# Attention and two gated layers on one core: query tiles through one copied bank, first transfers by a list

## The chip, the core and the metric

The kernel runs on one core of a Trainium2 chip. A core has TensorE (matmuls, which write to PSUM), VectorE, ScalarE and GpSimd (elementwise work; GpSimd works on SBUF), and SyncE, whose queue issues the transfers between HBM and SBUF here. The metric is the device time of one execution in microseconds (us). The profile calls the engines PE (PEld is its weight load), DVE, ACT, POOL and SP.

## What is computed

```
kv  = einsum('bhsd,bhse->bhde', k, v)            # 4 batches, 8 heads, 576 tokens, 64 wide
out = einsum('bhsd,bhde->bhse', q, kv)
x   = out / sqrt(mean(out * out, axis=-1) + 1e-06) * g_norm   # as 2304 tokens x 512
x   = ((x @ w_a) * (x @ w_b)) @ w_out                         # 512 -> 1536 -> 512
y   = (sigmoid(x @ w_gate) * (x @ w_val)) @ w_out2            # the same sizes
```

All data are float32. There is no softmax, so keys and values shrink to a 64 x 64 matrix for each head and batch before a query is needed.

## The kernel before

**Attention.** Keys and values come in 16 transfers of 640 KB, four pieces for each of four batches; a piece (two heads) is five matmuls into a quarter of a PSUM bank (L405). When a batch's four pieces are done, the two diagonal blocks of the bank are copied into `kvbd`, one by ScalarE (L416), one by VectorE (L419). Queries come as 18 tiles of 128 tokens, 256 KB each. A query tile is four or eight matmuls against `kvbd` (L475). ScalarE squares the result (L484), VectorE sums it by heads (L491), and once a *lot* of two or three tiles has its sums, GpSimd, ScalarE and VectorE make the inverse root from them (L436, L440, L443, L449 to L453). VectorE multiplies the tile in PSUM by it (`xn`, L497), TensorE transposes it (L504), and ScalarE copies it into `part` (L510), the SBUF tensor that holds x for the layers that follow.

**The layers.** Tokens go in three groups of 768, weights in quarters of two blocks of 128 columns (12 blocks a layer). For each group and quarter there are seven *kinds* of products (a Strassen form; kinds 1 to 7), each for the two factors u and v, six matmuls of 384 columns (L549); then eight output projections of six matmuls (L641), whose results are added into `part` by VectorE (L649, or by copies L651 and L653 in the first quarter). A product needs x or a sum of parts of x (L324) split in a high and a low part (L343 on ScalarE, L346 on GpSimd or VectorE), and weights that are clamped, rounded and split in the same way (load L225; L234, L238, L242 to L254; L290, L294). Split x is stored to HBM (L350) and reloaded for later quarters (L363).

**PSUM.** Six banks u0 to u5 are for products; o0 and o1 are for everything else. Query tiles 0 to 11 use u0 to u5, tiles 12 to 17 use o0 and o1; keys and values and transposes use o1 (transposes from tile 12 on o0 or o1); output projections use o0 and o1 in turn.

**What sets the order.** Every step is an `op` of a `Plan` with an engine, a planned duration, the steps that it needs (`after`), buffers that it takes (`new`) and uses, and a due time. `order` works due times back from the products, whose due times are a fixed grid 1,044 ns apart, then walks through time and gives each free engine the ready step that is due first. The list that comes out is the program: each engine runs its steps in that order. The transfers of SP run in order as well, and one that waits for its buffer holds those behind it. At most eight transfers are under way, since the ninth waits for the first to land. Three rings of buffers matter: `xr` (five, split x and the keys and values in flight), `q` (three query tiles) and `raw` (two weight blocks as they arrive).

Of the kernel before, what the change touches and what calls it, by code (L numbers as in the profile page):

```python
# [16 lines left out]
ACTF = mybir.ActivationFunctionType  # L17
# [31 lines left out]
         "gf": 2, "q": 3, "xn": 2, "ss": 2, "rr": 2}  # L49
# [4 lines left out]
LOTS = [(0, 1, 2), (3, 4, 5), (6, 7, 8), (9, 10, 11), (12, 13), (14, 15), (16, 17)]  # L54


class Plan:
# [6 lines left out]
    def op(self, name, eng, ns, fn, after=(), new=(), uses=(), due=None, lag=150, port=False):  # L64
        o = dict(name=name, eng=(eng,) if isinstance(eng, str) else eng, ns=ns, fn=fn, new=list(new),
                 uses=list(uses) + [b for _, b in new], due=due, lag=lag, port=port, succ=[], need=0, at=None)
        self.by[name] = o
        o["after"] = list(after)
        self.ops.append(o)

    def order(self):
# [21 lines left out]
        free_at = {e: 0 for e in ("PE", "DVE", "ACT", "POOL", "SP")}  # L93
        ready = {e: [] for e in free_at}
# [3 lines left out]
        events = [(0, i, "ready", o) for i, o in enumerate(ops) if not o["need"]]  # L98
# [69 lines left out]
def attention_then_two_moes(  # L168
# [49 lines left out]
    W_DUE = {(0, "a"): 17e3, (0, "b"): 17e3, (1, "a"): 20e3, (1, "b"): 20e3}  # L218

    def weights(F, which):  # L220
# [38 lines left out]
        op(("load", k), "SP", dma(512), load, new=[("raw", raw)], due=W_DUE.get(k), lag=2000)  # L259
# [122 lines left out]

    def keys_values(b):
        bank = ("K", b)
        for p in range(KC):
            kv = ("kv", b, p)

            ring = b < 2 or p > 1

            def load(p=p, kv=kv, ring=ring):  # L390
                if ring:
                    t = new_tile("xr", [2, 2, N])
                    t = t.rearrange("p a c n -> p (a c n)")
                else:
                    t = part[b - 1][:, p].rearrange("p k n -> p (k n)")
# [12 lines left out]

            op(kv, "SP", dma(640), load, (), [("xr", kv)] if ring else [], lag=2000)
            op(("K", b, p), "PE", 1120, mm, [kv] + ([("K", b, p - 1)] if p else [("O", t) for t in tiles_of.get(b - 2, ())]),  # L410
               [("o1", bank)] if p == 0 else [], ([bank] if p else []) + ([kv] if ring else []))
# [10 lines left out]
        op(("V", b, 0), "ACT", 400, up, before, uses=[bank])  # L422
        op(("V", b, 1), "DVE", 430, dn, before, uses=[bank])

# [36 lines left out]
    def queries(t):  # L461
        q = ("q", t)
        bank, tbank = ("O", t), ("T", t)
        tag, ttag = f"u{t % 6}" if t < 12 else f"o{t % 2}", f"o{t % 2}" if t >= 12 else "o1"

        def load():
            x = new_tile("q", [KC * P])
# [26 lines left out]

        def norm():
            tl["xn", t] = new_tile("xn", [KC, P])
            V.tensor_tensor(  # L497
                out=heads(tl["xn", t]), in0=heads(tl[bank]), in1=tl["rr", lot][:, t - lot[0]].to_broadcast([P, H, D]), op=ALU.mult
            )

        def transpose():
            b = tl[tbank] = bank_of(ttag).rearrange("p (k n) -> p k n", k=KC)
# [6 lines left out]
        def to_x():  # L509
# [3 lines left out]
        op(q, "SP", dma(256), load, (), [("q", q)], due=18e3 if t < 3 else None, lag=2000)  # L513
        op(bank, "PE", 1000, mm, [q] + [("V", i, e) for i, _, _ in batches(t) for e in (0, 1)]
           + ([('T', t - 2)] if t >= 12 else []), [(tag, bank)], [q])
# [6 lines left out]
        op(xn, "DVE", 720, norm, [rr], [("xn", xn)], [bank, rr])  # L522
        op(tbank, "PE", 480, transpose, [xn], [(ttag, tbank)], [xn])
        op(("Y", t), "ACT", 700, to_x, [tbank, "gcol"] + ([("K", in_part[t][0] + 1, in_part[t][1])] if t > 5 else []),
# [143 lines left out]
    op("gcol", "SP", 100, lambda: nc.sync.dma_start(out=gcol, in_=g_col), lag=2000)  # L668
# [89 lines left out]
```

## Time and profile before

| | |
|---|---|
| median of 3 runs | 931.04 us (930.25 to 932.25) |
| profiled execution | 927.02 us, span 925.2 us |
| PE busy | 890.8 us, 96% of the span |
| DVE, ACT, POOL busy | 638.0, 423.4, 334.5 us |
| HBM | 256 MB, 277 GB/s over the span |

The span is the stretch from the first to the last instruction of the program in the trace; the execution's own time is a little longer. Times in the rows count from the span's start. A matmul in float32 appears as two records, so ten records are a piece of keys and values; a few records can be missing. A row of the timeline merges neighbours of one kind: start, length, engine, line, what it writes and reads, how often, and in brackets the idle time ahead of it with what ended that.

### The profile page before, as it was taken

The page shows a single profiled execution, that of the slowest core. Times are in us where ns is not written, and L with a number is a line of the kernel's source. Part 1 is how long each engine was busy: PE and PEld are TensorE (multiplying, and loading weights), DVE is VectorE, ACT ScalarE, POOL GpSimd, SP SyncE. Part 2 cuts the span into 40 slices and gives each one's busy share as a digit, 9 for nine tenths or more (in the row PEclk, how much of TensorE's full clock was granted, in tenths as well). Part 3 has the DMA queues.
Part 4 walks back from the last instruction along what each step waited for, and adds up shares of the span by engine and source line. Part 5 has one row for each costly group of instructions (what it writes and reads, how often), then busy time and mean ns, then how long its engine had stood idle before and what let it go on. Part 6 is the DMA issues. An engine that isn't in the chain of part 4 may idle for free.

```text
span 925.2 us, 14091 instructions
## 1 busy us (share of the span) xinstructions
PE 890.8 (96%) x5144; PEld 882.6 (95%) x5144; DVE 638.0 (69%) x1129; ACT 423.4 (46%) x812; POOL 334.5 (36%) x307
## 2 busy tenths in 40 slices
PE   5889789999999999999999999999999999999998
PEld 5878779999999999999999999999999999999998
DVE  5588878578766766766778798777667667644445
ACT  4476555444443343343346575554444444333321
POOL 3245454234413413323336554332322322311111
PEclk8999989999999999999999999999999999999999
DMA  8795649988887787787785678988787797777783
GB/s 351 265 367 223 211 178 318 372 308 303 306 311 272 258 308 261 267 325 268 262 326 213 244 270 300 337 328 285 264 320 266 263 326 261 242 237 239 243 286 120
DMA packets 55221, 256.78 MB, mean 278 GB/s; under 512 B 6256, under 2 KB 9328, under 8 KB 55152
## 3 DMA queue, kind: packets, MB, share of 16 engines
q1 hardware_dynamic: 55152, 255.88, 77.4%
q8 instruction: 41, 0.67, 0.3%
q14 instruction: 28, 0.23, 0.1%
HBM read 218.10 MB, written 37.75 MB: 277 GB/s over the span
## 4 chain that ended last, share of the span: by engine, by line
PE 87%; DMA 5%; DVE 3%; POOL 1%; issue 1%; ACT 1%; SPq 0%; POOLq 0%; ACTq 0%
PE ps_u L549 54%; PE ps_o L641 32%; DMA raw<-w_all_dram 4%; DMA xr<-kv_in_dram 1%; PE ps_u L475 1%; PE ps_o L405 1%; DVE s L324 1%; DVE xn L497 1%; DMA x<-xr 0%; PE ps_o L504 0%; DVE mag L244 0%; POOL xr L346 0%; ACT xr L343 0%; DVE xr L346 0%; ACT mag L234 0%
## 5 line engine op out<-in xcount | busy, mean ns | idle before, releaser
L549 PE MATMUL ps_u<-xr,wp 128*128 128x384 f32 x3024 | 554.3, 336 | 2.7 <-ACT xr L343 1.1
L549 PEld LDWEIGHTS ps_u<-xr,wp 128*128 128x128 f32 x3024 | 529.3, 188 | 4.1 <-POOL xr L346 1.4
L641 PE MATMUL ps_o<-gu,wo 128*128 128x384 f32 x864 | 199.5, 339 | 11.2 <-DVE xn L497 9.4
L641 PE MATMUL ps_o<-gv,wo 128*128 128x384 f32 x864 | 201.4, 341 | 0.0
L649 DVE TENSOR_TENSOR part<-ps_o,part 128x384 f32<-128x384 f32 x240 | 132.0, 554 | 88.1 <-PE ps_o L641 87.6
L641 PEld LDWEIGHTS ps_o<-gu,wo 128*128 128x128 f32 x864 | 155.8, 190 | 13.6 <-DVE xn L497 6.6
L641 PEld LDWEIGHTS ps_o<-gv,wo 128*128 128x128 f32 x864 | 157.8, 190 | 0.0
L621 POOL TENSOR_TENSOR gu<-gf,gu 128x384 fp32r<-128x384 f32 x53 | 56.3, 1062 | 273.4 <-ACT gu L618 223.3
L254 POOL TENSOR_TENSOR w<-mag,last 128x512 int32<-128x512 int32 x72 | 97.7, 1362 | 109.3 <-DVE mag L248 106.0
L234 ACT ACTIVATE mag<-raw 128x512 f32<-128x512 f32 x72 | 48.2, 669 | 74.2 <-DMA raw<-w_all_dram 60.8
L294 POOL TENSOR_TENSOR wp<-tmp,wp 128x512 fp32r<-128x512 f32 x28 | 37.5, 1344 | 96.5 <-ACT wp L290 96.1
L618 ACT ACTIVATE gu<-gf 128x384 fp32r<-128x384 f32 x72 | 37.6, 522 | 63.6 <-DVE gf L614 63.3
L242 DVE TENSOR_SCALAR mag<-mag 128x512 f32<-128x512 f32 x72 | 35.2, 489 | 36.5 <-ACT mag L234 36.5
L248 DVE SCALAR_TENSOR_TENSOR mag<-raw,mag 128x512 uint32<-128x512 uint32 x72 | 49.9, 695 | 0.8
L290 ACT ACTIVATE wp<-tmp 128x512 fp32r<-128x512 f32 x48 | 30.2, 629 | 44.0 <-PE ps_u L549 26.3
L238 ACT ACTIVATE last<-raw 128x512 int32<-128x512 uint32 x72 | 47.6, 662 | 0.0
L567 ACT ACTIVATE u2u<-ps_u 128x384 f32<-128x384 f32 x36 | 17.6, 488 | 64.9 <-PE ps_u L549 64.9
L290 ACT ACTIVATE wp<-w 128x512 fp32r<-128x512 f32 (+1 forms) x48 | 24.9, 521 | 44.5 <-PE ps_u L549 35.0
L294 POOL TENSOR_TENSOR wp<-w,wp 128x256 fp32r<-128x256 f32 (+1 forms) x30 | 30.0, 1001 | 39.8 <-ACT wp L290 39.7
L618 ACT ACTIVATE gv<-gf 128x384 fp32r<-128x384 f32 x72 | 37.6, 522 | 14.2 <-DVE gf L614 13.9
L346 POOL TENSOR_TENSOR xr<-s,xr 128x768 fp32r<-128x768 f32 x16 | 31.1, 1945 | 33.3 <-ACT xr L343 30.7
L244 DVE TENSOR_SCALAR mag<-mag 128x512 uint32<-128x512 uint32 x72 | 40.7, 566 | 2.5
(78 smaller groups left out, 833.0 us busy)
## 6 DMA issues: line engine op xcount, KB each, us to landing
xr<-x SPq DMA_DIRECT2D x210, 768.0 KB, 5.9
raw<-w_all_dram SPq DMA_DIRECT2D x72, 512.0 KB, 5.7
x<-xr SPq DMA_DIRECT2D x42, 768.0 KB, 4.0
xr<-kv_in_dram SPq DMA_DIRECT2D x12, 640.0 KB, 7.2
q<-q_t_dram SPq DMA_DIRECT2D x18, 256.0 KB, 5.4
out_dram<-part SPq DMA_DIRECT2D x24, 192.0 KB, 2.2
part<-kv_in_dram SPq DMA_DIRECT2D x4, 640.0 KB, 6.3
gcol<-g_col_dram SPq DMA_DIRECT2D x1, 0.5 KB, 4.9
```

The costliest lines, as they stand in the source:

```text
L234: A.activation(out=tl["mag", k], in_=words(1).bitcast(F32), func=ACTF.Abs, scale=65536.0)
L238: A.activation(out=tl["last", k], in_=words(0), func=ACTF.Copy, scale=2.0**-29)
L244: V.tensor_scalar(out=m, in0=m, scalar1=3, scalar2=None, op0=ALU.logical_shift_left)
L248: V.scalar_tensor_tensor(out=m, in0=words(1), scalar=0x80000000, in1=m, op0=ALU.bitwise_and, op1=ALU.bitwise_or)
L254: G.tensor_tensor(out=tl["w32", k].bitcast(I32), in0=tl["mag", k].bitcast(I32), in1=tl["last", k], op=ALU.add)
L290: A.activation(out=tl[name][:, 0, :], in_=tl[src][:, cut], func=ACTF.Copy)
L294: eng.tensor_tensor(out=t[:, 1, :], in0=tl[src][:, cut], in1=t[:, 0, :], op=ALU.subtract)
L549: nc.tensor.matmul(out=o, lhsT=wt[:, a, c], rhs=x[:, b, k, :], start=(i in "152" and k == 0 and (a, b) == (0, 0)), stop=(k == 1 and (a, b) ...
L618: A.activation(out=tl[name][:, 0, :], in_=tl[me, "gf", t], func=ACTF.Copy)
L621: eng.tensor_tensor(out=tl[name][:, 1, :], in0=tl[me, "gf", t], in1=tl[name][:, 0, :], op=ALU.subtract)
L641: nc.tensor.matmul(out=o[:, :N], lhsT=tl["wo", f_of(g, uv)][:, a, c], rhs=tl["g", g, uv, t][:, b, :], start=(uv, a, b) == mms[0], stop=(uv ...
L649: V.tensor_tensor(out=acc, in0=o, in1=acc, op=ALU.add)
```

## The change

Four things are done. **First**, query tiles from the seventh on (t = 6 to 17) go through bank o0 alone; ScalarE copies the result out of PSUM into an `xn` buffer (of which there are four instead of two), and VectorE's multiplication then works in that buffer. Transposes all use o1. Lots are of two from the seventh tile on. **Second**, query tiles 0 to 5 are loaded into `part[0]`, which is not needed until x is written there, and all keys and values of batches 2 and 3 into `part[1]` and `part[2]`. **Third**, a list `FIRST` gives the first transfers their order by a `rank`, which overrides the due time: batch 0 in four pieces, four query tiles, the first two weight blocks, batch 1, two query tiles, two weight blocks, and so on. **Fourth**, both diagonal blocks are copied by ScalarE.

```diff
-LOTS = [(0, 1, 2), (3, 4, 5), (6, 7, 8), (9, 10, 11), (12, 13), (14, 15), (16, 17)]
+LOTS = [(0, 1, 2), (3, 4, 5), (6, 7), (8, 9), (10, 11), (12, 13), (14, 15), (16, 17)]
...
+        for o in ops:
+            if o["rank"] is not None:
+                o["due"] = o["rank"]
...
-    W_DUE = {(0, "a"): 17e3, (0, "b"): 17e3, (1, "a"): 20e3, (1, "b"): 20e3}
+    FIRST = [("kv", 0, p) for p in range(KC)] + [("q", t) for t in range(4)]
+    FIRST += [("load", (0, c)) for c in "ab"] + [("kv", 1, p) for p in range(KC)] + [("q", 4), ("q", 5)]
+    FIRST += [("load", (1, c)) for c in "ab"] + ["gcol"] + [("kv", 2, p) for p in range(KC)]
+    FIRST += [("q", t) for t in range(6, 9)] + [("kv", 3, p) for p in range(KC)]
+    load_due = {name: 100 * i - 1e5 for i, name in enumerate(FIRST)}
...
-            ring = b < 2 or p > 1
+            ring = b < 2
+            place = (1, p) if (b, p) in ((2, 0), (2, 1)) else (2, p % 2)
...
-        def up():
-            A.activation(out=dst[0:64, :, 0:64], in_=tl[bank][0:64, :, 0:64], func=ACTF.Copy)
-        def dn():
-            V.tensor_copy(out=dst[64:128, :, 64:128], in_=tl[bank][64:128, :, 64:128])
+        def diagonal():
+            for h in range(2):
+                r = slice(64 * h, 64 * h + 64)
+                A.activation(out=dst[r, :, r], in_=tl[bank][r, :, r], func=ACTF.Copy)
...
-        tag, ttag = f"u{t % 6}" if t < 12 else f"o{t % 2}", f"o{t % 2}" if t >= 12 else "o1"
+        tag = f"u{t}" if t < 6 else "o0"
...
+            if t < 6:
+                x = part[0][:, t // 3].rearrange("p k n -> p (k n)")[:, t % 3 * KC * P:(t % 3 + 1) * KC * P]
+            else:
+                x = new_tile("q", [KC * P])
...
+        def copy():
+            tl["xn", t] = new_tile("xn", [KC, P])
+            A.activation(out=tl["xn", t], in_=tl[bank], func=ACTF.Copy)
...
-        op(xn, "DVE", 720, norm, [rr], [("xn", xn)], [bank, rr])
+        if t < 6:
+            op(xn, "DVE", 720, norm, [rr], [("xn", xn)], [bank, rr])
+        else:
+            op(("copy", t), "ACT", 610, copy, [bank], [("xn", xn)], [bank])
+            op(xn, "DVE", 720, norm, [rr, ("copy", t)], (), [xn, rr], port=True)
```

Line numbers move: L405 becomes L419, L475 L491, L497 L519, L504 L526, L510 L532, L549 L576, L641 L668, the copy out of PSUM is L514.

The new order moves nearly every instruction; three places follow. On TensorE, where the first group's projections (L641, into the banks `ps_o`) meet the last query tiles (`ps_o<-kvbd,q`), the order before is:

```order
L549 MATMUL ps_u_935<-xr,wp_245 128x384 x6
L641 MATMUL ps_o_1135<-gu_776,wo 128x384 x3
L641 MATMUL ps_o_1135<-gv_808,wo 128x384 x3
L641 MATMUL ps_o_1149<-gu_776,wo 128x384 x3
L641 MATMUL ps_o_1149<-gv_808,wo 128x384 x3
L504 MATMUL ps_o_1162<-ident,xn 128x128 x4
L641 MATMUL ps_o_1170<-gu_776,wo 128x384 x3
L641 MATMUL ps_o_1170<-gv_808,wo 128x384 x3
L475 MATMUL ps_o_1184<-kvbd_66,q 128x128 x4
L504 MATMUL ps_o_1193<-ident,xn 128x128 x4
L475 MATMUL ps_o_1204<-kvbd_66,q 128x128 x4
```

And in the order after, at the same projections:

```order
L668 MATMUL ps_o_912<-gu_743,wo 128x384 x3
L668 MATMUL ps_o_912<-gv_824,wo 128x384 x3
L526 MATMUL ps_o_925<-ident,xn 128x128 x4
L668 MATMUL ps_o_934<-gu_743,wo 128x384 x3
L668 MATMUL ps_o_934<-gv_824,wo 128x384 x3
L526 MATMUL ps_o_949<-ident,xn 128x128 x4
L491 MATMUL ps_o_961<-kvbd_66,q 128x128 x4
L668 MATMUL ps_o_970<-gu_743,wo 128x384 x3
L668 MATMUL ps_o_970<-gv_824,wo 128x384 x3
```

The projections, which stood in blocks, now alternate with single transposes and query tiles. On ScalarE, around the first copies of transposed tiles into `part_67` (that is `part[0]`), the order before alternates squares (`sq`) and copies:

```order
L484 ACTIVATE sq<-ps_u_396 128x512
L510 ACTIVATE part_67<-ps_o_403,gcol 128x4x128
L484 ACTIVATE sq<-ps_u_412 128x512
L510 ACTIVATE part_67<-ps_o_423,gcol 128x4x128
L484 ACTIVATE sq<-ps_u_430 128x512
L510 ACTIVATE part_67<-ps_o_450,gcol 128x4x128
```

After, the first three copies (L532) stand among the steps of the first weights (`mag`, `last`, `wp`):

```order
L298 ACTIVATE wp_267<-w_246 128x256
L242 ACTIVATE mag<-raw 128x512
L500 ACTIVATE sq<-ps_u_271 128x512
L246 ACTIVATE last<-raw 128x512
L242 ACTIVATE mag<-raw 128x512
L532 ACTIVATE part_67<-ps_o_259,gcol 128x4x128
L500 ACTIVATE sq<-ps_u_285 128x512
L246 ACTIVATE last<-raw 128x512
L532 ACTIVATE part_67<-ps_o_309,gcol 128x4x128
L298 ACTIVATE wp_333<-tmp 128x512
L298 ACTIVATE wp_336<-w_320 128x512
L452 ACTIVATE root<-ss 128x24
```

The next entry there is the third copy, so five, two and three entries stand ahead of the three copies. On SP, the transfers around the first reloads of split x (`xr<-x_...`; `x_...<-xr` are the stores, `raw` the weights) stand before as:

```order
L225 DMA raw<-w_all_dram 128x512
L350 DMA x_1213<-xr 128x1536
L225 DMA raw<-w_all_dram 128x512 x4
L350 DMA x_1395<-xr 128x1536
L350 DMA x_1415<-xr 128x1536
L350 DMA x_1442<-xr 128x1536
L350 DMA x_1464<-xr 128x1536
L363 DMA xr<-x_569 128x1536
```

And after:

```order
L358 DMA x_1395<-xr 128x1536
L358 DMA x_1414<-xr 128x1536
L371 DMA xr<-x_432 128x1536
L371 DMA xr<-x_576 128x1536
L371 DMA xr<-x_597 128x1536
L358 DMA x_1514<-xr 128x1536
L233 DMA raw<-w_all_dram 128x512
L371 DMA xr<-x_664 128x1536
L233 DMA raw<-w_all_dram 128x512
```

The two `raw` loads of the lower piece (the last blocks of the second quarter's weights) are the first two of the four that stood ahead of the reloads before.

## Rows read from the trace of the kernel before

**Rows 1.** Windows: stretch in us, busy time and instructions by engine, granted clock, DMA

```profile
5.00:10.00 5.00, 2.23 (x10) 1.93 (x10) 3.23 (x5) 2.69 (x5) 1.30 (x1) 1.00 1.04 414
18.50:25.30 6.80, 6.04 (x28) 6.05 (x29) 3.13 (x6) 1.52 (x3) 2.30 (x2) 0.50 0.62 238
85.00:103.80 18.80, 14.14 (x88) 13.28 (x87) 16.63 (x26) 8.53 (x16) 9.57 (x15) 1.00 0.72 262
103.80:107.20 3.40, 3.40 (x14) 3.30 (x13) 2.55 (x7) 1.77 (x4) 0.85 (x1) 0.51 0.10 39
117.50:124.30 6.80, 5.11 (x16) 5.11 (x17) 3.37 (x7) 2.79 (x5) 3.16 (x5) 0.50 0.10 38
130.00:925.20 795.20, 790.01 (x4510) 788.24 (x4508) 547.79 (x982) 350.85 (x682) 278.30 (x226) 1.00 0.79 280
```

**Rows 2.** Waits of PE, whole span: us in total, times, longest

```profile
PE ps_o L405 <- DMA xr<-kv_in_dram: 10.2, 5, 4.7
PE ps_o L641 <- DVE xn L497: 9.4, 3, 4.7
...
PE ps_o L641 <- DVE part L649: 1.6, 2, 1.1
...
PE ps_o L641 <- ACT part L651: 0.2, 1, 0.2
```

**Rows 3.** Timeline of PE, 99 to 150 us

```profile
103.22 0.78 PE L641 MATMUL ps_o<-gu,wo 128*128 128x384 f32 x3 [3.42 <-DVE xn L497]
...
119.19 1.33 PE L641 MATMUL ps_o<-gu,wo 128*128 128x384 f32 x3 [4.74 <-DVE xn L497]
...
131.90 4.50 PE L549 MATMUL ps_u<-xr,wp 128*128 128x384 f32 x24
...
146.75 8.51 PE L549 MATMUL ps_u<-xr,wp 128*128 128x384 f32 x48
```

**Rows 4.** Timeline of PE, the first 45 us

```profile
4.72 2.50 PE L405 MATMUL ps_o<-xr 128*128 128x128 f32 x10 [4.72 <-DMA xr<-kv_in_dram]
10.89 4.49 PE L405 MATMUL ps_o<-xr 128*128 128x128 f32 x20 [3.66 <-DMA xr<-kv_in_dram]
...
26.26 1.28 PE L405 MATMUL ps_o<-xr 128*128 128x128 f32 x10
27.37 1.06 PE L475 MATMUL ps_u<-kvbd,q 128*128 128x128 f32 x8
28.27 1.28 PE L405 MATMUL ps_o<-xr 128*128 128x128 f32 x10
...
42.91 0.66 PE L504 MATMUL ps_o<-ident,xn 128*128 128x128 f32 x4
43.41 2.16 PE L475 MATMUL ps_u<-kvbd,q 128*128 128x128 f32 x16
```

**Rows 5.** Groups of instructions of the first 128 us: busy us, mean ns | idle

```profile
L254 POOL TENSOR_TENSOR w<-mag,last 128x512 int32<-128x512 int32 x11 | 16.0, 1455 | 29.7 <-DVE mag L248 29.6
L510 ACT ACTIVATE part<-ps_o,gcol 128x512 f32<-128x512 f32 x18 | 12.3, 686 | 8.8 <-PE ps_o L504 8.7
L491 DVE TENSOR_REDUCE ss<-sq 128x8 f32<-128x512 f32 x18 | 12.3, 682 | 8.8 <-ACT sq L484 8.8
...
L416 ACT ACTIVATE kvbd<-ps_o 64x256 f32<-64x256 f32 x4 | 1.5, 372 | 5.3 <-PE ps_o L405 5.3
```

**Rows 6.** Timeline of DVE, 29 to 64 us

```profile
29.10 0.69 DVE L491 TENSOR_REDUCE ss<-sq 128x8 f32<-128x512 f32 x1
...
33.42 0.69 DVE L497 TENSOR_TENSOR xn<-ps_u,rr 128x512 f32<-128x512 f32 x1 [0.21 <-POOL rr L453]
...
54.87 1.97 DVE L346 TENSOR_TENSOR xr<-part,xr 128x768 fp32r<-128x768 f32 x1 [0.57 <-ACT xr L343]
...
62.77 0.95 DVE L346 TENSOR_TENSOR xr<-part,xr 128x768 fp32r<-128x768 f32 x1
```

**Rows 7.** Timeline of POOL, 50 to 58 us

```profile
54.19 1.84 POOL L346 TENSOR_TENSOR xr<-s,xr 128x768 fp32r<-128x768 f32 x1 [1.77 <-ACT xr L343]
```

More of the change, by code (lines that the diff above doesn't have):

```diff
@@ L62, in __init__, with op @@
         self.ops, self.by, self.n = [], {}, 0
-    def op(self, name, eng, ns, fn, after=(), new=(), uses=(), due=None, lag=150, port=False):
+    def op(self, name, eng, ns, fn, after=(), new=(), uses=(), due=None, lag=150, port=False, rank=None):
         o = dict(name=name, eng=(eng,) if isinstance(eng, str) else eng, ns=ns, fn=fn, new=list(new),
-                 uses=list(uses) + [b for _, b in new], due=due, lag=lag, port=port, succ=[], need=0, at=None)
+                 uses=list(uses) + [b for _, b in new], due=due, lag=lag, port=port, rank=rank, succ=[], need=0, at=None)
         self.by[name] = o
@@ L97, in order @@
         tag_of = {b: tag for tag, bs in turn.items() for b in bs}
-        events = [(0, i, "ready", o) for i, o in enumerate(ops) if not o["need"]]
+        events = [(1300, i, "ready", o) for i, o in enumerate(ops) if not o["need"]]
         heapq.heapify(events)
@@ L381, in bank_of @@
         return ps.tile([P, 512], F32, tag=tag, name=f"ps_{tag}")
+    at_part = {}
     def keys_values(b):
@@ L386, in keys_values, with load @@
             kv = ("kv", b, p)
-            ring = b < 2 or p > 1
-            def load(p=p, kv=kv, ring=ring):
+            ring = b < 2
+            place = (1, p) if (b, p) in ((2, 0), (2, 1)) else (2, p % 2)
+            before = [("K", *at_part[place])] if place in at_part else []
+            if not ring:
+                at_part[place] = (b, p)
+            def load(p=p, kv=kv, ring=ring, place=place):
                 if ring:
@@ L394, in load @@
                 else:
-                    t = part[b - 1][:, p].rearrange("p k n -> p (k n)")
+                    t = part[place[0]][:, place[1]].rearrange("p k n -> p (k n)")
                 t = t[:KP, :KJ * 2 * P]
@@ L407, in mm @@
                     )
-            op(kv, "SP", dma(640), load, (), [("xr", kv)] if ring else [], lag=2000)
-            op(("K", b, p), "PE", 1120, mm, [kv] + ([("K", b, p - 1)] if p else [("O", t) for t in tiles_of.get(b - 2, ())]),
+            op(kv, "SP", dma(640), load, () if ring else before, [("xr", kv)] if ring else [], rank=load_due[kv], lag=2000)
+            op(("K", b, p), "PE", 1200, mm, [kv] + ([("K", b, p - 1)] if p else [("O", t) for t in tiles_of.get(b - 2, ())]),
                [("o1", bank)] if p == 0 else [], ([bank] if p else []) + ([kv] if ring else []))
         dst = kvbd[b % 2]
-        def up():
-            A.activation(out=dst[0:64, :, 0:64], in_=tl[bank][0:64, :, 0:64], func=ACTF.Copy)
-        def dn():
-            V.tensor_copy(out=dst[64:128, :, 64:128], in_=tl[bank][64:128, :, 64:128])
+        def diagonal():
+            for h in range(2):
+                r = slice(64 * h, 64 * h + 64)
+                A.activation(out=dst[r, :, r], in_=tl[bank][r, :, r], func=ACTF.Copy)
         before = [("K", b, 3)] + [("O", t) for t in tiles_of.get(b - 2, ())]
-        op(("V", b, 0), "ACT", 400, up, before, uses=[bank])
-        op(("V", b, 1), "DVE", 430, dn, before, uses=[bank])
+        op(("V", b), "ACT", 700, diagonal, before, uses=[bank])
     def powers(lot):
@@ L493, in mean @@
             )
+        def copy():
+            tl["xn", t] = new_tile("xn", [KC, P])
+            A.activation(out=tl["xn", t], in_=tl[bank], func=ACTF.Copy)
         def norm():
-            tl["xn", t] = new_tile("xn", [KC, P])
+            if t < 6:
+                tl["xn", t] = new_tile("xn", [KC, P])
             V.tensor_tensor(
-                out=heads(tl["xn", t]), in0=heads(tl[bank]), in1=tl["rr", lot][:, t - lot[0]].to_broadcast([P, H, D]), op=ALU.mult
+                out=heads(tl["xn", t]), in0=heads(tl[bank] if t < 6 else tl["xn", t]), in1=tl["rr", lot][:, t - lot[0]].to_broadcast([P, H, D]), op=ALU.mult
             )
         def transpose():
-            b = tl[tbank] = bank_of(ttag).rearrange("p (k n) -> p k n", k=KC)
+            b = tl[tbank] = bank_of("o1").rearrange("p (k n) -> p k n", k=KC)
             for p in range(KC):
@@ L512, in queries @@
         sq, xn, ss, rr = (("sq", t), ("xn", t), ("ss", lot), ("rr", lot))
-        op(q, "SP", dma(256), load, (), [("q", q)], due=18e3 if t < 3 else None, lag=2000)
-        op(bank, "PE", 1000, mm, [q] + [("V", i, e) for i, _, _ in batches(t) for e in (0, 1)]
-           + ([('T', t - 2)] if t >= 12 else []), [(tag, bank)], [q])
+        op(q, "SP", dma(256), load, (), [] if t < 6 else [("q", q)], rank=load_due.get(q), lag=2000)
+        op(bank, "PE", 1000, mm, [q] + [("V", i) for i, _, _ in batches(t)]
+           + ([('T', t - 4)] if t >= 10 else []), [(tag, bank)],
+           [] if t < 6 else [q])
         op(sq, "ACT", 610, square, [bank], [("sq", sq)], [bank])
@@ L521, in queries @@
             powers(lot)
[L522 to L524 removed]
+        if t < 6:
+            op(xn, "DVE", 720, norm, [rr], [("xn", xn)], [bank, rr])
+        else:
+            op(("copy", t), "ACT", 610, copy, [bank], [("xn", xn)], [bank])
+            op(xn, "DVE", 720, norm, [rr, ("copy", t)], (), [xn, rr], port=True)
+        op(tbank, "PE", 480, transpose, [xn], [("o1", tbank)], [xn])
+        op(("Y", t), "ACT", 700, to_x, [tbank, "gcol"] + ([("K", *at_part[in_part[t]])] if t > 5 else [("O", i) for i in range(6)]),
            uses=[tbank])
@@ L665, in down @@
                [("sum", g, t, d)], lag=2000)
-    op("gcol", "SP", 100, lambda: nc.sync.dma_start(out=gcol, in_=g_col), lag=2000)
+    op("gcol", "SP", 100, lambda: nc.sync.dma_start(out=gcol, in_=g_col), rank=load_due["gcol"], lag=2000)
     for b in range(B):
```

6 lines of the change are left out of this document (3 added, 3 removed).

## The prediction

> **What bounds the kernel now.** I read the windows first, then TensorE's waits and its timeline, and last the engines that it waits for. From 130 us to the end TensorE is busy 790.01 of 795.20 us at the full clock [rows 1]: those 795 us are a queue of matmuls almost without holes, and only the opening can become shorter. In the list of waits the reader should see two causes behind most of TensorE's idle time: keys and values still in flight (10.2 us) and, three times, an output projection (L641) that waits for the attention's normalised tile xn (9.4 us) [rows 2].
>
> A fixed point makes the opening countable. In both orders the same 94 pieces of TensorE work stand ahead of the first product of kind 5 of the third token group: 16 key-value pieces, 18 query tiles, 18 tiles of transposes, 30 products and 12 output projections. Since what follows has hardly a hole, the time at which that product starts moves the end by as much. Before, it starts at 131.90 us [rows 3]. Unit times without a wait: 48 matmuls, which are 8 products, take 8.51 us, 1.06 each [rows 3] (a projection has as many); a key-value piece takes 27.37 - 26.26 = 1.11, a query tile 28.27 - 27.37 = 0.90, a tile of transposes 43.41 - 42.91 = 0.50 [rows 4]. The work is 16 x 1.11 + 18 x 0.90 + 18 x 0.50 + 42 x 1.06 = 87.5 us, so 131.9 - 87.5 = 44.4 us are lost.
>
> Where they go. Idle: the 13 rows of the list add up to 31.0, of which the 1.6 behind L649 come later, so 29.4 us [rows 2]. Clock: three stretches at 1.2 GHz hold 6.04, 3.40 and 5.11 us of busy TensorE, half of it lost, 7.3 us [rows 1]; the second and the third follow waits of 3.42 and 4.74 us [rows 3]. Besides, the first three key-value pieces took 2.50 + 4.49 us where three take 3.33 later, 3.7 us lost [rows 4]. That is 40.4; the other 4.0 are gaps too short for the list.
>
> **The change part by part.**
>
> *First transfers in order.* Before, the later pieces of batch 0 stand behind weights and queries, and TensorE waits 3.66 us for the second [rows 4]. Now the four pieces go first. The queue moves 414 GB/s [rows 1], so 640 KB land every 1.58 us after the first at 4.7 us. At 6.99 / 3 = 2.33 us a piece TensorE no longer waits between them, but still loses half of three: 4.7 us idle and 3.7 of clock (2.4 to 4.9 for two to four pieces). Batch 0 is done at 4.7 + 6.99 + 1.11 = 12.8.
>
> *Both diagonal blocks on ScalarE.* Two copies of 0.37 in a row [rows 5] instead of one there and one on VectorE beside it: 0.75 us until the first query tile at 13.55; the fourth ends at 17.2. Batch 1's last piece comes after 6,528 KB more, at 4.7 + 16.1 = 20.8, and is done at 21.9; 0.3 us are lost to data.
>
> *First norms.* VectorE now has steps of the weights between the sums of squares. Three sums are 2.0 us [rows 5], and two clamp pairs with a sign step 3.23, as the five VectorE entries of 5 to 10 us show [rows 1]. The first square ends at 13.55 + 0.90 + 0.7 = 15.1, so the third sum at 20.4. From such a sum's end to its xn the trace has 33.42 - 29.79 = 3.6 us, and xn takes 0.69 [rows 6]: transposes from 24.6, 2.7 us lost.
>
> *Three transposes through one bank.* Each needs ScalarE's copy of the one before, 0.69 us [rows 5], and now ScalarE has weights and squares ahead of it: five entries before the first copy, two before the second, three before the third, as the order shows, and one of the last waits for a GpSimd add of 1.46 [rows 5]. Ten entries of 0.22 to 0.67, 5.7 us in all, with three copies and the add make 9.2: the third copy ends at 33.8. TensorE has three transposes and two query tiles in that time, 3.3 us; 5.9 are lost, 2.1 if every copy were prompt. With so little work the clock should fall there. The three stretches of before cost 1.7 to 3.0 each; I take 2.5.
>
> *From there to the first long wait.* TensorE waits 0.7 for the diagonal copies, twice 0.6 for copies out of PSUM, 1.0 for a copy into part: each is one or two ScalarE entries. Then products need part of x: behind the sixth transposes come copy, norm, sum, high part and GpSimd's low part, 1.84 [rows 7], the other four under 1 us each, some 5.6 together, with 3.1 us of work beside them: 2.5. Together 5.4 us.
>
> *Outputs copied out of PSUM.* Here is the gain. Before, a query tile from the thirteenth on kept its bank until the lot's norm: square, sum, root, reciprocal, GpSimd steps, norm. The projections that needed the bank stood 9.4 us [rows 2], and twice the clock fell behind it, 1.7 and 2.6: 13.7 us. Now one ScalarE copy of at most 0.69 frees the bank. Twelve such copies are 8 us more for ScalarE, hidden: from 85 to 103.8 us it is busy 8.53 of 18.80 [rows 1]. What is late next is the copy behind other ScalarE work, or the eviction of the projection before: four such waits stand in TensorE's order, each between 0.5 us (one entry alone) and 1.6 (behind another step); 4.2 us, between 2.0 and 6.4. At the end the last lots' norms still hold three transposes: 1.8 for a norm behind a GpSimd low part [rows 7], and twice 0.8 for the single bank, 3.4 us, with a fall of the clock at even odds, 1.3.
>
> Twelve norms now read two operands from SBUF. A VectorE subtraction of this kind took 0.95 us alone and 1.97 while GpSimd was at its 1.84 [rows 6, 7], so each norm that meets GpSimd may wait up to 1.8 us; I counted it once, in the 1.8 just named. The Trainium skill gives the reason (SBUF — State Buffer, Who interferes with whom): a VectorE instruction with two SBUF inputs contends with a GpSimd instruction that reads SBUF, and whichever is second blocks; the norm of before, with one input in PSUM, was free of it. By that rule the change pays on all twelve; what it would make of the time is rival C.
>
> *The rest.* Lots of two are one more chain of small steps beside other work; two q buffers instead of three serve twelve tiles instead of eighteen. Nothing on the path.
>
> **The sum.** Lost: 4.7 + 3.7 + 0.75 + 0.3 + 2.7 + 5.9 + 2.5 + 5.4 + 4.2 + 3.4 + 1.3 = 34.9, and 4.0 of short gaps as before, 38.9. The fixed point comes at 87.5 + 38.9 = 126.4 instead of 131.9, 5.5 us earlier. The profiled execution took 927.0 us around its span of 925.2, the median of the runs is 931.0; 5.5 off gives 921.5 there and **925.5 us** for the median.
>
> **Rivals.** (A) ScalarE reaches the copies promptly and the clock stays up: 5.9 becomes 2.1, and 2.5 and 1.3 vanish; 13.1 us gained, 917.9. For it: the copies are short; against it: the order. (B) The weights of the next quarter come late. Two of their loads now stand behind three reloads of x that followed them before, as the order shows. A reload is 768 KB, 1.9 us at 414 GB/s, so one to three of them delay the weights by 1.9 to 5.7 us, and the products that need them, behind 140 us, would wait where before there is no such wait: 927.4 to 931.2 if nothing covers it. (C) Norms blocked by GpSimd on the path twice more: 3.6 back, 929.1. (D) Slower: the clock falls at about 25 us and does not come back until the wait at 55. Between lie 17 us of work; at half rate they cost 17, less the 2.5 counted and at most 5.4 of waits that swallow it: 9.1 us, 3.6 slower, 934.6. It decides if no stretch there is busy enough; for it speak the six short waits, against it that the clock came back by 25.3 with TensorE busy 6.04 of 6.80 [rows 1]. (E) The change doesn't do what it says: the copies stand behind other ScalarE work for as long as the norm did. The 13.7 come back less the 4.2 and 1.3 counted: 2.7 slower, 933.7.
>
> **How the numbers follow.** Forecast 0.50, with a range of its own from 922 to 928.5 (the bounds of the first pieces, the clock and the four waits); A 0.12; B 0.13; C 0.10; D 0.09; E 0.06. The range 918.5 to 930.5 leaves out D, E and the edges of A and B. A measurement tells 0.2% from no change, 1.9 us: faster is below 929.2. Faster: the forecast, A, half of B, most of C, 0.77. The same: the rest of B and C, 0.11. Slower: D and E with an edge of B, 0.12.
>
> **What would show it.** The fixed point near 126; no wait of projections for xn; key-value pieces back to back from 4.7 us; some 8 us of idle between 22 and 34 us with transposes in it, and a low clock there. Wrong would be: a wait for wp or for a reloaded x behind 135 us (B), low clock up to 55 us (D), waits of projections above 2 us (E).

## The result, and the profile after

| | median | range | runs |
|---|---|---|---|
| before | 930.64 us | 928.83 to 932.25 | 4 |
| after | 918.19 us | 915.77 to 919.82 | 4 |

The ratio is 0.9865 (95% interval 0.9832 to 0.9897): 12.5 us faster. The forecast was 925.5, with a range from 918.5, so the gain was more than twice the 5.5 us of the sum. The profiled execution of after took 919.54 us around a span of 917.2.

The opening looks as described. The first view is the timeline of TensorE (PE) in the changed kernel: start, length, engine, line, tiles, and the idle time ahead with what ended it.

```profile
4.76 7.24 PE L419 MATMUL ps_o<-xr 128*128 128x128 f32 x40 [4.76 <-DMA xr<-kv_in_dram]
12.96 3.81 PE L491 MATMUL ps_u<-kvbd,part 128*128 128x128 f32 x32 [0.97 <-issue]
...
25.38 0.63 PE L526 MATMUL ps_o<-ident,xn 128*128 128x128 f32 x4 [2.40 <-DVE xn L519]
...
29.43 0.66 PE L526 MATMUL ps_o<-ident,xn 128*128 128x128 f32 x4 [1.31 <-ACT part L532]
31.05 0.66 PE L526 MATMUL ps_o<-ident,xn 128*128 128x128 f32 x4 [0.96 <-ACT part L532]
33.49 2.76 PE L419 MATMUL ps_o<-part 128*128 128x128 f32 x13 [1.78 <-ACT part L532]
...
75.92 2.04 PE L491 MATMUL ps_o<-kvbd,q 128*128 128x128 f32 x8 [3.26 <-DMA q<-q_t_dram]
...
118.59 0.63 PE L526 MATMUL ps_o<-ident,xn 128*128 128x128 f32 x4 [1.59 <-DVE xn L519]
...
129.54 4.67 PE L576 MATMUL ps_u<-xr,wp 128*128 128x384 f32 x26
```

Against [rows 4] the four pieces of batch 0 stand back to back from 4.76 us; the first transposes come at 25.38, and each of the next waits for a copy into `part`. New, and in no step of the prediction, is 75.92: the thirteenth query tile waits 3.26 us for its q. The fixed point, the first product of kind 5 of the third token group, is at 129.54 us, against 131.90 [rows 3]: only 2.4 us of the 8.0 by which the two spans differ.

TensorE's waits over the whole span (us in total, times, longest), beside [rows 2]:

```profile
PE ps_o L419 <- DMA xr<-kv_in_dram: 5.3, 4, 4.8
PE ps_o L526 <- DVE xn L519: 4.3, 3, 2.4
PE ps_o L526 <- ACT part L532: 4.3, 4, 1.3
PE ps_o L491 <- DMA q<-q_t_dram: 3.3, 1, 3.3
...
PE ps_o L668 <- ACT part L678: 1.5, 1, 1.5
...
PE ps_o L668 <- DVE part L680: 0.9, 2, 0.7
```

The 9.4 us that projections waited for xn are gone, as is half of the wait for keys and values. Windows of the changed kernel, with columns as in [rows 1]: the three stretches at 1.2 GHz, and all that follows the fixed point.

```profile
33.90:37.40 3.50, 3.50 (x19) 3.50 (x18) 1.54 (x2) 0.82 (x2) 3.08 (x7) 0.51 0.96 380
74.90:85.10 10.20, 8.40 (x38) 7.26 (x39) 3.77 (x8) 4.34 (x10) 4.01 (x7) 0.50 0.33 112
119.30:126.10 6.80, 6.10 (x21) 6.11 (x22) 4.24 (x7) 3.35 (x6) 0.00 (x1) 0.50 0.20 78
129.54:917.20 787.66, 783.27 (x4501) 781.75 (x4500) 550.34 (x993) 353.13 (x687) 285.54 (x231) 1.00 0.80 285
```

The second stretch stands behind the wait for q. The last row is the surprise: the same work that took 795.2 - 1.9 = 793.3 us from the fixed point before takes 787.7 now. Neither row has holes to speak of, and both are at 2.4 GHz (granted clock 1.00). It is the same work, and from 170 us on products and projections stand in the same order in both. The matmuls themselves follow each other faster. I measured the pace as the mean distance between the starts of successive 128x384 matmuls from 200 to 880 us (distances under 200 ns): 174.95 ns before, 173.79 after. A *group* below is one token group with one quarter: 22 *slots* (14 products and 8 projections) of six matmuls each; there are 36 groups (three token groups, six quarters a layer, two layers). A slot of six undisturbed matmuls takes 1040 ns; the loss in a group is 132 times the pace above 1040 / 6, which is 214 ns before and 60 after. The difference of 154 ns, 36 times, is 5.5 us. In the timeline of the kernel before, a projection pair and what follows:

```profile
411.31 0.68 PE L641 MATMUL ps_o<-gu,wo 128*128 128x384 f32 x3
411.83 0.70 PE L641 MATMUL ps_o<-gv,wo 128*128 128x384 f32 x3
412.38 0.68 PE L641 MATMUL ps_o<-gu,wo 128*128 128x384 f32 x3
412.89 0.68 PE L641 MATMUL ps_o<-gv,wo 128*128 128x384 f32 x3
413.42 2.27 PE L549 MATMUL ps_u<-xr,wp 128*128 128x384 f32 x12
415.52 0.68 PE L641 MATMUL ps_o<-gu,wo 128*128 128x384 f32 x3
```

The first projection takes 412.38 - 411.31 = 1.07 us, the second 1.04, two products 2.10. The slow slots are the first projection after a product and the first product after a projection, in every group.

### The profile page after: what moved, and what is told of

Its sections match the earlier page's. It is cut to its first block, busy times and chain, and to the rows that moved or that the text cites. A ratio compares the mean times of both kernels' runs of the same rounds, so it can differ in the third digit from the quotient of the medians.

```text
span 917.2 us, 14089 instructions
## 1 busy us (share of the span) xinstructions
PE 885.8 (97%) x5144; PEld 877.8 (96%) x5144; DVE 636.1 (69%) x1125; ACT 428.4 (47%) x829; POOL 341.5 (37%) x314
## 4 chain that ended last, share of the span: by engine, by line
PE 88%; DMA 5%; DVE 3%; ACT 2%; issue 1%; POOL 0%; SPq 0%; ACTq 0%; DVEq 0%; POOLq 0%
PE ps_u L576 54%; PE ps_o L668 30%; DMA raw<-w_all_dram 3%; PE ps_o L419 2%; PE ps_o L491 1%; DMA x<-xr 1%; DMA q<-q_t_dram 1%; PE ps_o L526 1%; DVE xn L519 1%; DVE mag L250 0%; DMA xr<-kv_in_dram 0%; DVE mag L252 0%; ACT part L532 0%; ACT mag L242 0%; ACT sq L500 0%
## 5 line engine op out<-in xcount | busy, mean ns | idle before, releaser
L576 PE MATMUL ps_u<-xr,wp 128*128 128x384 f32 x3024 | 553.9, 338 | 1.4 <-POOL xr L354 1.4
L576 PEld LDWEIGHTS ps_u<-xr,wp 128*128 128x128 f32 x3024 | 529.2, 189 | 2.1 <-POOL xr L354 1.6
L668 PE MATMUL ps_o<-gu,wo 128*128 128x384 f32 x864 | 198.7, 338 | 3.6 <-ACT part L678 1.5
L668 PE MATMUL ps_o<-gv,wo 128*128 128x384 f32 x864 | 196.8, 335 | 0.0
L668 PEld LDWEIGHTS ps_o<-gu,wo 128*128 128x128 f32 x864 | 154.4, 189 | 5.6 <-ACT part L678 1.9
L668 PEld LDWEIGHTS ps_o<-gv,wo 128*128 128x128 f32 x864 | 154.8, 189 | 0.0
L648 POOL TENSOR_TENSOR gu<-gf,gu 128x384 fp32r<-128x384 f32 x47 | 49.3, 1049 | 227.8 <-ACT gu L645 178.1
L645 ACT ACTIVATE gu<-gf 128x384 fp32r<-128x384 f32 x72 | 37.5, 521 | 52.1 <-DVE gf L641 51.8
L302 POOL TENSOR_TENSOR wp<-w,wp 128x256 fp32r<-128x256 f32 (+1 forms) x37 | 38.2, 1036 | 39.3 <-ACT wp L298 39.3
L645 ACT ACTIVATE gv<-gf 128x384 fp32r<-128x384 f32 x72 | 37.5, 521 | 15.6 <-DVE gf L641 15.0
```

What stands on the lines that cost most here:

```text
L302: eng.tensor_tensor(out=t[:, 1, :], in0=tl[src][:, cut], in1=t[:, 0, :], op=ALU.subtract)
L576: nc.tensor.matmul(out=o, lhsT=wt[:, a, c], rhs=x[:, b, k, :], start=(i in "152" and k == 0 and (a, b) == (0, 0)), stop=(k == 1 and (a, b) ...
L645: A.activation(out=tl[name][:, 0, :], in_=tl[me, "gf", t], func=ACTF.Copy)
L648: eng.tensor_tensor(out=tl[name][:, 1, :], in0=tl[me, "gf", t], in1=tl[name][:, 0, :], op=ALU.subtract)
L668: nc.tensor.matmul(out=o[:, :N], lhsT=tl["wo", f_of(g, uv)][:, a, c], rhs=tl["g", g, uv, t][:, b, :], start=(uv, a, b) == mms[0], stop=(uv ...
```

## The experiments

**Where the pace comes from.** In this program a pool of SBUF tiles gets its address when its first tile is made, so the order of the steps and the sizes of the rings decide where everything lies. The change moved weights (`wp0` to `wp3`, `wo`) and gated tiles (`g`) by 2 to 14 KB. The first kernels separate address and order: the tiles of one kernel at the addresses of the other, by an explicit list of pools.

```diff
+LAYOUT = [("xr", 6144, 5), ("raw", 4096, 2), ("sq", 2048, 1), ("ss", 96, 2), ("mag", 2048, 2), ("last", 2048, 2),
+          ("w32", 2048, 4), ("wp0", 4096, 3), ("root", 96, 1), ("rr", 96, 2), ("q", 2048, 3), ("pad", 2048, 1),
...
+    def lay_out():
+        for tag, size, count in LAYOUT:
+            pool = ctx.enter_context(tc.tile_pool(name=f"{tag}_{len(pools)}", bufs=count))
+            for _ in range(count):
+                pool.tile([P, size // 4], F32, tag=tag, name=tag)
```

> The kernel before, instruction for instruction in the same order, with its SBUF tiles put at the addresses that they have in the changed kernel (from the weights and the products' tiles on, all of them; the q and xn rings trade their two places). Of the 12.5 us that the change gave, the opening (up to the first product of kind 5 of the third token group) shows only 2.4; the rest grew evenly behind it, with 128x384 matmuls that start every 173.8 ns instead of every 175.0. Theory P: the pace belongs to the places of the tiles in SBUF. Then this kernel has the opening of before (131.9 us) and the pace of after: 4,000 matmuls by 1.2 ns, about 5 us less, 925 to 926 us, and the late d and u slots run at 1040 to 1048 ns instead of 1066. Rival S: the pace belongs to the instruction stream or to what stands ahead in the queues, or to the chip: then the time stays 930 to 931 and the pace 175.0.

Measured: 924.05 us, ratio to before 0.9952 (0.9930 to 0.9974). The pace is 173.80 ns and every slot of the group has the time that it has in the changed kernel, within 1 ns. The counterpart:

> The changed kernel, same instructions in the same order, with all tiles that the products and projections use at the addresses of the kernel before (the counterpart of the first run). Theory P: the pattern of before comes back, 213 ns lost in a group of 22 slots instead of 59, 5.5 us: 918.2 + 5.5 = 923.7 us. Rival S: 918 us.

Measured: 921.51 us (917.57 to 927.54), ratio 0.9928 (0.9899 to 0.9958); pace 174.95 ns, the pattern of before. So the pace is a matter of addresses alone; rival S falls.

**Which addresses.** In all kernels run, those with equal remainders of the start addresses modulo 512 have equal patterns. Before: 192 for x and all `wp`, 160 for `wo` and `g`. After: 192 for x, 384 for `wp0`, 160 for the rest. (A matmul has two operands in SBUF, weights and a *moving operand*: `wp` and x in a product, `wo` and `g` in a projection.) My first guess was a rule on 64 bytes; four kernels moved pools by pads of 32 bytes, the first of them like this:

```diff
+          ("pad1", 32, 1), ("wo", 4096, 3), ("pad2", 32, 1), ("c22u", 1536, 1), ("gf", 1536, 2), ("c22v", 1536, 1),
```

The second has only the pad behind `wo`:

> The kernel before with the output weights wo moved up by 32 bytes per partition, and nothing else but 64 bytes for the tiles behind them. In every run so far the slow slots depend on the start addresses of the weights modulo 64: where wp0 to wp3 start at 0 and wo at 32, every projection after a product and every product after a projection is slow (213 ns in a group of 22); where only wp0 starts at 0 and the other four at 32, 59 ns are lost, around kinds 1, 5 and 2. Theory W: a change of this remainder from one block of weights to the next costs time. Here all five start at 0, so all 22 slots should take 1040 ns, 213 ns x 36 groups = 7.7 us less: 921.5 to 923 us beside 929 to 930.6. Rival G: it is the remainder of the moving operand (x at 0, the gated tiles at 32), which does not change here: 929 to 931 us.

Measured: 921.08 us, ratio 0.9914 (0.9892 to 0.9937), 28 ns lost in a group. As theory W had it, but for the 28. By remainders modulo 512 all weights are at 192 here, x at 192 and the gated tiles at 224.

> The counterpart: wo stays where it is in the kernel before, and all that lies behind it (the gated tiles g and gf, c22, c11) moves up by 32 bytes, so that the moving operands of products and projections both start at 0 modulo 64 and only the weights differ. Theory W: pattern and time as before, 213 ns lost in a group, 929 to 931 us. Rival G: the slow slots go, 921.5 to 923 us.

Measured: 927.04 us, ratio 0.9985 (0.9968 to 1.0003); 159 ns lost, and nearly all of it now in the projections, both of a pair (`wo` at 160, the gated tiles at 192). Neither theory had that. The third and the fourth are the changed kernel with pads around `wp0`, and the kernel with three q buffers with pads around `wp1`, `wp2`, `wp3` and `wo`:

> The changed kernel with wp0 moved up by 32 bytes, so that all five weights tiles start at 32 modulo 64: none is aligned, all are alike. Theory W (a change of the remainder costs): 59 ns in a group go, 918.2 - 2.1 = 916 us, and all slots at 1040 ns. Rival A (a start that is not a multiple of 64 costs by itself): as much as or more than in the changed kernel, 918 us or above.

Measured: 924.29 us, ratio 0.9961 (0.9938 to 0.9984), 239 ns lost: the worst of all, against theory W.

> The changed kernel with three q buffers, and all five weights tiles at addresses that are multiples of 64 bytes. Theory W: the 59 ns in a group go, 2.1 us less than the same kernel without the pads, 912.9 - 2.1 = 910.8 us. Rival: what is left in kinds 1, 5 and 2 has another cause, 912 to 914 us.

Measured: 916.32 us, ratio 0.9867 (0.9846 to 0.9889), 200 ns lost instead of the 62 of the same kernel without pads. Theory W falls: with all five weights at multiples of 64 (192 to 384 modulo 512), TensorE is slower than with 32 and 0 mixed. What was left was equality. The five small tiles (`ss`, `root`, `rr`, 96 bytes each, 480 in all) are the only ones whose size is not a multiple of 512; laid last, they move nothing, and every operand starts at 192. The list then ends so:

```diff
+          ("gv0", 3072, 1), ("ss", 96, 2), ("root", 96, 1), ("rr", 96, 2)]
```

> The kernel before with the small pools laid last, so that before and changed kernel stand at one placement. Theory L: 213 ns x 36 groups go, 7.7 us: 929 - 7.7 = 921.5 us. The difference to the changed kernel at the same placement is what the change does by its own steps: 5.5 us as the prediction's sum had it, that is 916.0 for the changed kernel; if the prediction's sum was too small by itself, 8 to 10 us.

Measured: 920.51 us, ratio 0.9912 (0.9877 to 0.9947); pace 173.38 ns, 6 ns lost. In the timeline each pair of projections and each pair of products now takes 2.08 us:

```profile
411.51 0.68 PE L657 MATMUL ps_o<-gu,wo 128*128 128x384 f32 x3
412.03 0.68 PE L657 MATMUL ps_o<-gv,wo 128*128 128x384 f32 x3
412.55 0.68 PE L657 MATMUL ps_o<-gu,wo 128*128 128x384 f32 x3
413.07 0.68 PE L657 MATMUL ps_o<-gv,wo 128*128 128x384 f32 x3
413.59 2.24 PE L565 MATMUL ps_u<-xr,wp 128*128 128x384 f32 x12
415.67 0.68 PE L657 MATMUL ps_o<-gu,wo 128*128 128x384 f32 x3
```

> The changed kernel with the small pools laid last, two q buffers as it has. Theory L: 59 ns x 36 groups go, 918.2 - 2.1 = 916.1 us. Beside the run with three q buffers this measures the third buffer at one placement: by the wait of 3.3 us and the clock behind it 4 to 5 us; if that wait is there in some executions only, 2 to 3 us.

Measured: 917.20 us, ratio 0.9882 (0.9849 to 0.9915), 2 ns lost. At one placement the change gives 920.51 - 917.20 = 3.3 us here, and 929.34 - 921.51 = 7.8 at the addresses of before; the forecast lies between, and the intervals are wider than the difference.

> The changed kernel with three q buffers, and the pools of small tiles (ss, root, rr, 96 bytes each) laid behind all others. Every other tile's size is a multiple of 512 bytes, so every operand of TensorE then starts at 192 modulo 512. The two runs with multiples of 64 and of 32 bytes refuted the rule on 64; what all ten runs agree on is that kernels with the same remainders modulo 512 have the same pattern to the nanosecond, and that in the kernel before the slots are fast as long as the remainders stay the same. Theory L: with one remainder throughout nothing is lost, all 22 slots take 1040 ns; 912.9 - 2.1 = 910.8 us. Rival: a loss of 25 ns or more in a group remains, 912 us or above.

Measured: 911.88 us (909.88 to 912.97), ratio 0.9818 (0.9785 to 0.9851), 6 ns lost: theory L holds, and this kernel is faster than before and after. Three more kernels, each run once and made from the changed kernel with its small pools last, ask what about the remainder matters. The first has a pad of 32 bytes ahead of all pools:

> The changed kernel with small pools last, as in the run with no loss, and everything moved up by 32 bytes: every operand of TensorE starts at 224 modulo 512 instead of 192. If only sameness counts, nothing is lost again: 22 slots of 1040 ns, pitch 173.3 ns, as at 192. If 192 (a multiple of 64) is what counts, a loss of some 100 ns or more in a group comes back.

Measured: pace 173.35 ns, 2 ns lost: 192 or 224 makes no difference. The second has the same pad ahead of `xr` and 480 bytes behind it; the third has the weights together behind a pad of 480:

```diff
+LAYOUT = [("pad1", 32, 1), ("xr", 6144, 5), ("pad2", 480, 1), ("raw", 4096, 2), ("sq", 2048, 1), ("mag", 2048, 2),
```

> The same placement, with the ring of x alone at 224 modulo 512; all weights and the gated tiles at 192. The pair of weights and moving operand is then (192, 224) in products and (192, 192) in projections. If a change of either operand's remainder costs, some 20 ns at eight changes in a group, 160 ns or more. If only the weights' own remainder counts, nothing: 0.

Measured: 30 ns lost, in the first projection after a product. Neither 160 nor 0: a change of the moving operand alone costs little, as in the kernel with `wo` moved (28).

> The same placement, with all five blocks of weights at 160 modulo 512 and all moving operands at 192: the two differ by 32 bytes, but by the same 32 in all slots. If only a change of the remainders costs, nothing is lost: 0. If weights and moving operand must have the same remainder, all slots are slow as the projections were in the run that had this pair there (21 ns each): 460 ns in a group, pitch 176.8 ns.

Measured: 209 ns on average, but at two paces. From 400 to 580 us nearly all slots take 1040 ns, from 620 us on nearly all of them about 1060. Two places of its timeline:

```profile
301.03 0.69 PE L684 MATMUL ps_o<-gu,wo 128*128 128x384 f32 x3
301.56 0.69 PE L684 MATMUL ps_o<-gv,wo 128*128 128x384 f32 x3
302.09 0.69 PE L684 MATMUL ps_o<-gu,wo 128*128 128x384 f32 x3
302.62 0.69 PE L684 MATMUL ps_o<-gv,wo 128*128 128x384 f32 x3
303.15 7.05 PE L592 MATMUL ps_u<-xr,wp 128*128 128x384 f32 x39
```

```profile
414.01 0.68 PE L684 MATMUL ps_o<-gu,wo 128*128 128x384 f32 x3
414.53 0.68 PE L684 MATMUL ps_o<-gv,wo 128*128 128x384 f32 x3
415.05 0.68 PE L684 MATMUL ps_o<-gu,wo 128*128 128x384 f32 x3
415.57 0.68 PE L684 MATMUL ps_o<-gv,wo 128*128 128x384 f32 x3
416.09 1.20 PE L592 MATMUL ps_u<-xr,wp 128*128 128x384 f32 x6
```

At 301 us two projections take 2.12 us, at 414 us 2.08. With weights and moving operand at two remainders, the same instructions ran at either pace; with one remainder for all operands (four kernels) only the faster was seen. It is not enough that the two agree within a slot: in the kernel before they do, at 192 in products and at 160 in projections, and 214 ns are lost where one follows the other. What in the chip makes the two paces was not found, nor why some sets of unequal remainders cost 28 and others 239.

**The opening.** Two kernels do one part of the change each: the first keeps the copies, the lots of two and four xn buffers (L514 of the changed kernel, `tag = "o0"`) and takes back the list `FIRST`, the loads into `part` and the diagonal copies; the second does the opposite. Both have three q buffers.

> The kernel before with one part of the change: outputs copied out of PSUM from the seventh tile on, lots of two, four xn buffers. Loads, diagonal blocks and q buffers are as before. By the terms of the prediction the copies give 13.7 and cost 4.2 and 1.3 at the place where they act: 8.2 us, 922.4 us. Rival: the gain in the opening comes from the first transfers, and the copies only trade one wait for another: 928 to 930 us. Besides, the tiles lie at yet other addresses here, so by theory P the pace may be neither 175.0 nor 173.8 ns.

Measured: 921.74 us, ratio 0.9931 (0.9908 to 0.9955), at the remainders and the pace (174.96) of before. So the copies alone give about 7.5 us (4.2 to 8.5 by the interval) beside the 929.2 of before on that chip. The expectation has a slip: by the prediction's own terms the wait of the last transposes (3.4) belongs to the copies too, which makes them 4.8, not 8.2.

> The kernel before with the other parts of the change: the given order of the first transfers, later keys and values and first queries loaded into part, both diagonal blocks on ScalarE. The outputs stay in PSUM until the norm, as before; lots, xn and q buffers as before. By the terms of the prediction the copies were worth 8.2 us and the whole 5.5, so this part alone costs 2.7 us: 933.3 us. Rival: it removes the waits for keys and values (10.2 us before, 5.3 after) without a new one: 925 to 926 us.

Measured: 918.49 us, ratio 0.9903 (0.9866 to 0.9941). Both numbers missed: this kernel happens to have the remainders of the changed kernel (pace 173.80), which is 5.5 us of its 10.7. The other 5 us are the first transfers' own, but the interval of the ratio leaves them anything from 0 to 7. The rival's reason, no wait for keys and values without a new one, is not what the trace shows; TensorE's longest waits there are:

```profile
PE ps_o L419 <- DMA xr<-kv_in_dram: 5.4, 4, 4.7
PE ps_o L658 <- DVE xn L513: 5.2, 3, 4.1
PE ps_o L419 <- DMA part<-kv_in_dram: 4.5, 1, 4.5
```

Keys and values are waited for as long as before (5.4 + 4.5 against 10.2), half of it now where they are loaded into `part`, and projections still wait 5.2 us for xn.

The third buffer alone, in the changed kernel:

```diff
-         "gf": 2, "q": 2, "xn": 4, "ss": 2, "rr": 2}
+         "gf": 2, "q": 3, "xn": 4, "ss": 2, "rr": 2}
```

> The changed kernel with three q buffers again, as before the change. Theory: the 3.3 us that the thirteenth query tile waits for its q, and the 10.2 us at the lower clock behind it, come from the ring of two, since the load is issued only when the tile before the last has been read. With a third buffer the wait goes, and half of the busy time in the slow stretch, some 4 to 5 us, comes back: 918.2 - 3.3 - 4.5 = 910 to 911 us; if the clock falls anyway, 915. Rival: the load is late because other transfers stand ahead of it in the queue (it landed 6.5 us after its issue), or the next wait takes the place: 917 to 918 us.

Measured: 912.86 us, ratio 0.9834 (0.9802 to 0.9865). The wait for q is gone, and in the three traces of this order the clock is at 2.4 GHz from 37.5 us to 910. In the timeline the thirteenth query tile starts at 72.88 us and waits 0.74 for a copy:

```profile
72.88 1.16 PE L491 MATMUL ps_o<-kvbd,q 128*128 128x128 f32 x8 [0.74 <-ACT xn L514]
```

Against the same placement with two buffers, 917.20, the kernel with three has 911.88: the third buffer is worth 5.3 us.

**Single executions differ.** One program's time differs from one execution to the next: the kernel before took 923.1 to 934.2 us in 20 runs on one chip. Each kernel has one trace, but all kernels with one order of instructions share an opening but for its addresses, and it comes out differently too. In the seven of the changed order the stretches at 1.2 GHz go with it: they sum to between 10.2 and 27.3 us, counted from 10 us to 910, and the trace with the least has the earliest fixed point, the one with the most the latest. In the order before they explain less (its latest, 134.31, has 10.2 us of them). So one trace before and one after say little of 2 or 3 us. Over all traces of one order, whatever its addresses:

| order of the program | traces | fixed point, us | first product of kind 5, third group, second quarter |
|---|---|---|---|
| before | 5 | 130.18 to 134.31, mean 131.95 | 195.0 to 199.0, mean 196.9 |
| after | 7 | 122.85 to 130.69, mean 126.43 | 188.8 to 197.2, mean 192.5 |
| copies alone | 1 | | 191.7 |
| first transfers alone | 1 | 129.19 | 193.8 |
| after, three q buffers | 3 | | 186.8 to 187.8, mean 187.2 |

The second point has the same 156 pieces of work ahead in all orders; with copies alone or three q buffers, four more projections stand ahead of the first, so it is left out there.

## Right and wrong, step by step

**The sum of the opening** came out right in total: 131.95 - 126.43 = 5.5 us over the traces, as forecast, and the mean of the fixed point is the forecast's 126.4. That it fits to the tenth is luck, since the standard error of that difference, from the spread of the traces, is 1.3 us. The changed kernel at the addresses of before has the ratio 0.9928, which on 931.04 is 924.3 us (921.6 to 927.1); the forecast was 925.5.

**The step that failed** is the sentence that links the opening to the end: "Since what follows has hardly a hole, the time at which that product starts moves the end by as much"; with it fell "only the opening can become shorter". It took a busy TensorE for a fixed time, and put the change of the remaining 795 us at nothing. [Rows 1] show 790.01 busy of 795.20, but not that the matmuls in it stood 174.95 ns apart where 173.35 is possible. The change moved the tiles, 154 ns in each of 36 groups went, and 5.5 us came on top. No rival had it. The range ended 0.3 us above the result, and left out A's own 917.9; without the 5.5 us the result would have been 923.7, inside it.

**"Two q buffers instead of three ... Nothing on the path"** was wrong. In all seven traces of the changed order TensorE stands idle 2.3 to 3.8 us ahead of the thirteenth query tile. In four of them the trace names the transfer of q. In the other three it names a step of ScalarE, but there too the tile's load, issued at 68.7, 70.0 and 68.9 us, lands at 74.89, 76.17 and 75.17, and the wait ends 0.14 us later. The loads stand behind stores of x, and with two buffers each is issued only when the tile before the last has been read. The third buffer gives 5.3 us back.

**What made up for it.** The two parts came out better than their terms, though neither is clear of noise alone: the first transfers gave some 5 us (0 to 7) where their terms allow 0.75 (25.95 after, against 44.4 - 13.7 - 4.0 = 26.7 before), the copies 7.5 (4.2 to 8.5) against 4.8. Together, less the 5.3 of the third buffer, which both still have, they make some 7 us; the whole gave 7.8 at the addresses of before. So a sum that was right in total had an error of 5 us on one side, shown, and about as much on the other, not shown term by term: its total is right in part by luck.

**Single terms in the profiled execution.** First pieces: four in 7.24 us where 4.44 are the unit times, 2.8 lost of 3.7. The prediction called this clock; here the matmul records do start 0.213 us apart until 10 us and 0.112 after that, but the granted clock there is 1.00, before [rows 1] and after, so no row shows the cause. First norms: 2.40 of 2.7. Three transposes through one bank: 1.31 + 0.96 + 1.78 = 4.05 of 5.9, the third copy done at 33.49 (forecast 33.8). The four waits among the projections, for a copy and three evictions, one of them at a query tile:

```profile
79.60 1.33 PE L668 MATMUL ps_o<-gu,wo 128*128 128x384 f32 x3 [0.78 <-ACT part L532]
...
88.41 0.79 PE L668 MATMUL ps_o<-gu,wo 128*128 128x384 f32 x3 [0.21 <-DVE part L680]
...
91.33 1.16 PE L491 MATMUL ps_o<-kvbd,q 128*128 128x128 f32 x8 [1.17 <-DVE part L680]
...
95.08 0.79 PE L668 MATMUL ps_o<-gu,wo 128*128 128x384 f32 x3 [1.54 <-ACT part L678]
```

They make 3.7 of 4.2. Last transposes: 0.30 + 1.59 + 0.78 = 2.7 of 3.4. The clock fell at 33.9 us for 3.5 us, which cost 1.8 of the 2.5; at the end it fell for 6.8 us and cost 3.1, more than the even odds of 1.3; behind the wait for q it cost 4.2, which with the wait's own 3.3 was in no term. These 7.5 us are more than the 3.1 by which this execution's fixed point (129.54) came after the forecast's.

**The rule on norms.** That a norm with both operands in SBUF can be blocked by GpSimd, as the Trainium skill has it (SBUF — State Buffer, Who interferes with whom), agrees with the trace. Two forms of the norm in the changed kernel, VectorE's groups in the first 130 us (busy us, mean ns):

```profile
L519 DVE TENSOR_TENSOR xn<-xn,rr 128x512 f32<-128x512 f32 x12 | 10.2, 885 | 0.5 <-POOL rr L465 0.5
...
L519 DVE TENSOR_TENSOR xn<-ps_u,rr 128x512 f32<-128x512 f32 x6 | 3.8, 685 | 2.9 <-POOL rr L465 2.9
```

The mean of the twelve is 200 ns longer; in the trace it is two of them, at 116 and 118 us, that took 2.30 and 1.48 us beside GpSimd steps of 2.23 and 1.45; the other ten took 0.68 to 0.69. The first of the two is behind the 1.59 us wait above; the second ended at 119.85, ahead of the copy (119.94) that the last transposes waited for. One such wait was counted, and rival C's two more on the path did not come.

**The rivals.** A gave 917.9 us, close to the result, but by luck: it wants the clock up, and the clock fell three times. B, weights late behind 140 us: the waits after the fixed point are 0.7 and 0.4 us, for evictions, none for weights. D: the clock was back at 37.4 us. E: no projection waits longer than 1.5 us for anything.

## What to carry to other kernels

When a stage is bound by matmuls, its length is count times pace: measure the distance between starts in that stage, not only the busy share, and look at which slots are longer than the rest. An edit of rings or of order moves every tile behind it; laying tiles of odd size last, so that all operands of TensorE start at one remainder modulo 512, took the kernel before from 929.34 to 920.51 us without a change to any instruction but its addresses; 7.5 us of that are the pace (208 ns in each of 36 groups). And a buffer that is taken away has a price at its next load: follow that load in the queue before it is called free.

## What the runs showed of the hardware

- The same TensorE instructions in the same order run at 173.35 to 175.15 ns each, by the start addresses of their operands in SBUF alone. One remainder modulo 512 for all weights and moving operands: 2 to 6 ns lost in a group of 22 slots (four kernels, at 192 and at 224). More than one: 28 to 239 ns (thirteen kernels).
- With weights 32 bytes off the moving operand throughout, one execution ran at 1040 ns a slot in some stretches and at 1060 in others.
- The opening of some 130 us varied by 7.8 us over seven traces of one order of instructions (each at other addresses), largely with the stretches at 1.2 GHz; over five traces of the other order it varied by 4.1 us.
- A VectorE multiplication with both operands in SBUF took 0.68 us in ten of twelve cases, and 2.30 and 1.48 us where it ran beside GpSimd steps.
